# Attention scores by 64 keys and all eight heads at once, in place of 128 keys and four heads

## The chip, the cores and the metric

The kernel runs on one core of a Trainium2 chip. The metric is the device time of one execution in microseconds (us); of several runs the median is given. TensorE is PE in the profile (PEld are its weight loads), VectorE is DVE, ScalarE is ACT, GpSimd is POOL, SyncE is SP.

## The reference

Eight batches of 576 tokens and 8 heads of 64 columns. Attention looks back over a window of 128 tokens and subtracts a distance times a slope of its own for each head; its output goes through a layer that mixes all tokens of a batch.

```python
scores = scale * np.matmul(q, k.transpose(0, 1, 3, 2))
slopes = 2.0 ** (-8.0 * (np.arange(H, dtype=np.float32) + 1) / H)
bias = slopes[:, None, None] * (-np.abs(rel).astype(np.float32))[None, :, :]
mask = (rel >= 0) & (rel < window)
scores = np.where(mask, scores + bias[None], -1000000000.0)
attn = softmax(scores)
x = np.matmul(attn, v)                       # then (B, S, H * D)
wq, wk = x @ w_q, x @ w_k
W_tok = scale * np.einsum('bsd,btd->bst', wq, wk)
mixed = np.einsum('bst,btd->bsd', W_tok, x)
out = np.maximum(mixed, 0.0) @ w_out
```

All inputs and the output are float32 in DRAM. The kernel works in float16 on chip.

## The kernel before

**Steps of a batch.** Loads (Lq, Lk, Lv; Lt for the last 64 tokens of two batches) cast to float16 on the way and are issued by GpSimd (lines 504 to 523); four loads of the first batch come as float32 by SyncE and are cast on VectorE or ScalarE. TQ and TT transpose q and k on TensorE, two row halves at a time, with `flip` (lines 602 to 648), and ETQ and ETT copy them out of PSUM into `qkT`. `add_unit` (lines 654 to 690) makes a *unit*: QK, the scores of 128 keys against the 256 queries that can see them, for four heads (two pairs `a`, and in a pair the heads `e` on the two row halves of TensorE), laid out with keys on partitions; EXP, one exponential over 128x1024 on ScalarE from PSUM into a tile `pt`; MUL, one product on VectorE with a table `bias` that holds the exponential of the distance term, and zero outside the window. The last key block has 192 queries and takes the last 64 keys along in the other 64 columns (`segs`, table `biasl`). So a batch has four key blocks `g` of two units `u`, eight units in all.

`add_pv` (lines 694 to 739) makes PV for one tile of 128 queries: for each of eight heads two matmuls of 128 keys, `pt` as the stationary operand and 65 columns of `vt` (64 of v, and a column of ones that yields the sum of the softmax) as the moving one; X divides by that sum on VectorE (lines 729 and 730). There are five such tiles for a batch, the last with 64 queries. Then come XT (transposes of x, copied out by EXT), WQ, WK, G (the product of `wkn` and x), MX (mixing) with RM (the relu), and OUT with the copy EO and the store DO.

**Who orders the work.** `add` lists every step with its dependencies, its cost on the engines that may do it and a due time; `Order.solve` (line 234) plans them: of the steps that can start within 0.11 us of the earliest on an engine it takes the one with the smallest due time. The due times stand in the table `WANT`, one for each step, and the default for a step without entry follows `STRIDE` for the batch. `SWITCH` is the cost that the plan gives to a change of TensorE's array shape (`mode`). The engines then run their instructions in the planned order. Copies out of PSUM (ETQ, EXT, EWQ, EG, EO, RM and so on) go to ScalarE or VectorE as the plan finds best. While the planned start is below `WARM`, `keep_busy` fills gaps of TensorE with matmuls on a zero tile `fill`. Stores of batches 1 to 5 (`LATE`) wait until all loads are issued; their buffers are 23 (`HELD`).

**Buffers.** `nat` (q and k as loaded) and `vt` are four batches deep, `qkT`, `x` and what follows two, `pt` five key blocks of two tiles; PSUM has four pairs of banks, and QK, PV, TQ, XT and MX take a pair each. A v load of tile `t` waits only for the two PV that read that tile four batches before.

**The costs** that the plan uses for the steps at hand:

```python
s = add("QK", b, f"{g}.{u}", w, pe(0.225), need, em, banks=2, mode=1)
x = add("EXP", b, f"{g}.{u}", w + 0.6, {"ACT": (0.92, 1.02)}, [s, *oldp], ex, frees=[s])
mul[b, g, u] = add("MUL", b, f"{g}.{u}", w + 1.6, DVE(0.68), [x, (mkb if g < 3 else mkbl)[u]], ml)
p = add("PV", b, qt, want, pe(0.48 if qt else 0.25), need + [sets[b % NV], zerop], em, banks=2)
```

**The mask.** GpSimd makes an identity matrix, a table of distances (iota) and, after VectorE has cast it, sets everything outside the window to a large number in two selects; ScalarE makes `bias` from it with eight exponentials.

Of the kernel before, what the change touches and what calls it, by code (L numbers as in the profile page):

```python
# [14 lines left out]
P = 128  # L15
# [12 lines left out]
NPT = 5  # L28
PTW = 1088

# [3 lines left out]
STRIDE = 15.2  # L34
# [10 lines left out]
    "ident": -41.18, "idh": 86.52, "iota": -19.88, "dist": -5.89, "zeros": 80.97, "zerop":  # L45
# [237 lines left out]
def kernel(  # L283
# [137 lines left out]
    def mk_ident(o):  # L421
        make_identity(nc, ident32)
# [588 lines left out]
```

## Time and profile before

| What | Value |
|---|---|
| Median of 3 runs | 141.11 us (140.55 to 141.18) |
| Profiled execution | 141.34 us, of which its span in the profile 139.5 us |
| TensorE's granted clock | 0.997 |
| Busy in the span: PE, PEld, DVE, ACT, POOL | 129.3, 81.2, 112.6, 115.2, 110.0 us |
| EXP: 64 on ACT | 62.2 us busy, 1034 ns each |
| MUL: 48 and 16 on DVE | 32.0 and 10.8 us busy, 684 and 683 ns each |
| QK: 320 matmuls, 64\*128 pieces | 22.1 us booked |
| PV: 512 and 64 matmuls, 128\*128 | 22.9 and 4.9 us booked |
| Loads of v: 32 and 4 on POOL | 30.1 and 3.8 us busy |

The profile is one execution of the program. Times are from the start of the span. A group's row gives line, engine, operation, output and inputs, shapes and count, then busy time, the mean of one in ns, and the idle time of the engine ahead of it with what ended it. For matmuls the shape begins with the piece of the array that is used (rows\*columns). Matmuls are pipelined: their booked durations overlap, so that how fast they pass is read from their starts. A row of the timeline merges instructions of one group that follow each other: start, time from the first start to the last end, and the count.

### The profile page before, as it was taken

The numbers are of one execution on the slowest core, as the hardware profiler recorded it, in microseconds if no ns is written. First come the engines' busy times: TensorE is split into PE (matmuls) and PEld (weight loads), VectorE is DVE, ScalarE is ACT, GpSimd is POOL, SyncE is SP. The second block draws the span as 40 slices with busy tenths as digits, with TensorE's granted clock in tenths as the row PEclk, the third lists the DMA queues.
The fourth block names the chain that finished last, engine by engine and source line by source line (L and its number), as shares of the span: only waits on it lengthen the run. The fifth ranks groups of instructions, "written<-read, shape, count | busy, mean of one in ns | idle before, by whom it ended". The sixth has DMA issues, their size and how long they took to land.

```text
span 139.5 us, 5462 instructions
## 1 busy us (share of the span) xinstructions
PE 129.3 (93%) x2344; PEld 81.2 (58%) x2344; DVE 112.6 (81%) x250; ACT 115.2 (83%) x175; POOL 110.0 (79%) x145
## 2 busy tenths in 40 slices
PE   6999859998999999988999999999999999999980
PEld 2345447554676367766757567765666666865530
DVE  6648997659987899989999998899999989984400
ACT  6176988399669999999999989999999999676660
POOL 7899988899995899999999999999977745600000
PEclk9999999999999999999999999999999999999998
DMA  4999999999999999999999999999999993730494
GB/s 98 184 180 154 158 153 168 152 146 154 188 215 206 158 159 153 156 155 155 154 156 153 157 156 155 159 153 156 156 215 413 358 327 144 260 153 5 167 320 189
DMA packets 117127, 25.12 MB, mean 180 GB/s; under 512 B 113072, under 2 KB 114096, under 8 KB 117104
## 3 DMA queue, kind: packets, MB, share of 16 engines
q0 software_dynamic: 110912, 20.32, 169.0%
q1 hardware_dynamic: 6192, 4.46, 10.8%
q8 instruction: 18, 0.29, 0.8%
q14 instruction: 5, 0.04, 0.1%
HBM read 29.62 MB, written 9.44 MB: 280 GB/s over the span
## 4 chain that ended last, share of the span: by engine, by line
PE 60%; DVE 16%; POOL 8%; ACT 6%; DMA 5%; issue 2%; ACTq 0%; POOLq 0%; DVEq 0%
PE pair L344 52%; PE pair L347 8%; DVE pt L687 6%; DMA nat<-in_q_dram 5%; POOL nat L506 4%; ACT pt L680 4%; DVE x L730 3%; POOL vt L521 1%; POOL natt L513 1%; DVE inv L729 1%; DVE xtl L730 1%; DVE wqT L353 1%; DVE qkT L359 1%; DVE rm L843 1%; ACT xT L357 1%
## 5 line engine op out<-in xcount | busy, mean ns | idle before, releaser
L680 ACT ACTIVATE pt<-pair 128x1024 f16<-128x1024 f32 x64 | 62.2, 1034 | 2.3 <-PE pair L344 1.7
L687 DVE TENSOR_TENSOR pt<-pt,bias 128x1024 f16<-128x1024 f16 x48 | 32.0, 684 | 2.5 <-ACT pt L680 2.3
L344 PE MATMUL pair<-wout_sb,rm 128*128 128x512 f16 (+1 forms) x132 | 31.7, 373 | 0.2
L521 POOL DMA_DIRECT2D vt<-in_v_dram x32 | 30.1, 995 | 1.6 <-DMA natt<-in_q_dram 0.8
L506 POOL DMA_DIRECT2D nat<-in_k_dram x30 | 29.1, 997 | 0.5 <-DMA nat<-in_k_dram 0.3
L506 POOL DMA_DIRECT2D nat<-in_q_dram x30 | 29.0, 987 | 0.4 <-DMA natt<-in_k_dram 0.4
L344 PEld LDWEIGHTS <-pt 128*128 128x128 f16 x576 | 20.5, 97 | 6.2 <-issue 2.6
L344 PE MATMUL pair<-vt,pt 128*128 128x65 f16 x512 | 22.9, 193 | 0.4 <-ACT pt L680 0.4
L730 DVE TENSOR_TENSOR x<-pair,inv 128x512 f16<-128x512 f32 x32 | 22.1, 692 | 1.1
L344 PE MATMUL pair<-qkT 64*128 64x256 f16 (+2 forms) x320 | 22.1, 250 | 0.6 <-ACT pt L680 0.3
L351 ACT COPY osb<-pair 128x512 f32<-128x512 f32 x29 | 17.0, 596 | 5.7 <-PE pair L344 5.5
L344 PEld LDWEIGHTS <-rm 128*128 128x128 f16 x132 | 11.3, 97 | 11.8 <-issue 1.7
L357 ACT COPY qkT<-pair 128x1024 f32<-128x1024 f32 (+1 forms) x12 | 11.4, 949 | 7.7 <-PE pair L347 7.7
L344 PE MATMUL pair<-fill 128*128 128x512 f16 x52 | 15.4, 430 | 1.8 <-DVE fill L487 1.2
L918 POOL DMA_DIRECT2D out_dram<-osb x20 | 11.2, 574 | 6.6 <-ACT osb L351 3.6
L344 PEld LDWEIGHTS <-qkT 64*128 64x128 f16 x320 | 11.1, 94 | 8.0 <-issue 5.2
L347 PE MATMUL pair<-identh,nat 64*128 64x64 f16 x512 | 10.7, 190 | 1.3 <-DMA nat<-in_q_dram 0.9
L347 PEld LDWEIGHTS <-nat 64*128 64x128 f16 x512 | 9.2, 95 | 4.0 <-DMA nat<-in_q_dram 1.3
L687 DVE TENSOR_TENSOR pt<-pt,biasl 128x1024 f16<-128x1024 f16 x16 | 10.8, 683 | 0.0
L344 PE MATMUL pair<-xT,wqq_sb 128*128 128x320 f16 (+1 forms) x64 | 10.5, 286 | 0.3 <-DVE xT L359 0.3
L357 ACT COPY xT<-pair 128x512 f32<-128x512 f32 (+1 forms) x14 | 7.4, 527 | 3.6 <-PE pair L347 2.9
L359 DVE COPY qkT<-pair 128x512 f16<-128x512 f16 (+2 forms) x14 | 9.3, 686 | 1.3 <-PE pair L347 1.1
(63 smaller groups left out, 165.5 us busy)
## 6 DMA issues: line engine op xcount, KB each, us to landing
out_dram<-osb POOLq DMA_DIRECT2D x20, 256.0 KB, 4.6
vt<-in_v_dram POOLq DMA_DIRECT2D x32, 128.0 KB, 5.9
nat<-in_k_dram POOLq DMA_DIRECT2D x30, 128.0 KB, 6.0
nat<-in_q_dram POOLq DMA_DIRECT2D x30, 128.0 KB, 6.1
out_dram<-osb SPq DMA_DIRECT2D x11, 256.0 KB, 2.3
out_dram<-osb POOLq DMA_DIRECT2D x6, 128.0 KB, 4.2
natf<-in_q_dram SPq DMA_DIRECT2D x2, 256.0 KB, 4.7
natf<-in_k_dram SPq DMA_DIRECT2D x2, 256.0 KB, 5.4
```

What stands on the lines that cost most here:

```text
L344: hold(nc.tensor.matmul(*a, **k))
L347: hold(nc.tensor.transpose(*a))
L351: hold(nc.scalar.copy(out_ap, in_ap))
L353: hold(nc.vector.tensor_copy(out=out_ap, in_=in_ap))
L357: hold(nc.scalar.copy(out_ap.bitcast(FP32), in_ap.bitcast(FP32)))
L359: hold(nc.vector.tensor_copy(out=out_ap, in_=in_ap))
L506: return lambda: nc.gpsimd.dma_start(out=nat_s[b % NNAT][j][n], in_=src[b, :, P * n:P * n + P, :].transpose([1, 0, 2]))
L521: return lambda: nc.gpsimd.dma_start(out=vt_s[b % NV][t][:, :, 0:D], in_=v[b, :, P * t:P * t + P, :].transpose([1, 0, 2]))
L680: nc.scalar.activation(out=pt[:, 0:1024], in_=two(s.bank).rearrange("p e c -> p (e c)"), func=AF.Exp, scale=SCALE)
L687: ENG2[o.eng].tensor_tensor(out=pt[:, 0:1024], in0=pt[:, 0:1024], in1=bt, op=ALU.mult)
L730: nc.vector.tensor_tensor(out=x[r].rearrange("p (g h d) -> p g h d", g=2, h=4), in0=pxv[r, :, :, 0:64], in1=inv[r].unsqueeze(3).broadcast_ ...
L918: q.dma_start(out=out[b, P * st:P * st + P, c], in_=osb)
```

## The change

A unit now holds 64 keys against the 192 queries that can see them, for all eight heads: heads 0 to 3 on partitions 0 to 63, heads 4 to 7 on partitions 64 to 127, so 768 columns where there were 1024. QK uses 64x64 pieces of TensorE, four to a set (`x` the column half, `e` the row half). There are still eight units for a batch; the last takes key blocks 7 and 8 (128 and 64 queries). PV works by row halves: for each pair of head `h` and head `4 + h` two matmuls of 64 keys, four key blocks to a query tile. The tile `pt` is laid out with 64 zero columns ahead of each head's 192. v is loaded by head pairs with all tokens of the batch: four loads for a batch, each 64 partitions by 18 rows of 64, in place of four tiles of 128 tokens and a tail for two batches; every load of v waits for all PV of four batches before, and every PV waits for all four. The mask is made on VectorE by arithmetic in place of the selects on GpSimd, and the identity by a comparison of the iota with zero. All due times in `WANT` are new, `STRIDE` is 13.2 where it was 15.2. The rest of the batch (TQ, XT, WQ, WK, G, MX, OUT) stays.

```diff
-NPT = 5
+NPT = 10
+W = 192
-STRIDE = 15.2
+STRIDE = 13.2
...
+    def mk_idh(o):
+        nc.vector.tensor_scalar(out=identh, in0=wint[:, 0:P], scalar1=0.0, scalar2=1.0,
+                                op0=ALU.is_equal, op1=ALU.mult)
     def mk_dist(o):
-        nc.vector.tensor_copy(out=wm, in_=wint)
+        for x in range(2):
+            r = slice(64 * x, 64 * x + 64)
+            nc.vector.tensor_copy(out=wm[r], in_=wint[r, 64 * x:64 * x + W])
+        nc.vector.tensor_scalar(out=wlo, in0=wm, scalar1=-1.0e9, scalar2=0.0, op0=ALU.mult, op1=ALU.add)
+        nc.vector.tensor_scalar(out=whi, in0=wm, scalar1=-127.5, scalar2=1.0e9, op0=ALU.add, op1=ALU.mult)
+        nc.vector.tensor_tensor(out=wm, in0=wm, in1=wlo, op=ALU.max)
+        nc.vector.tensor_tensor(out=wm, in0=wm, in1=whi, op=ALU.max)
+        nc.vector.tensor_scalar(out=wm[64:128], in0=wm[64:128], scalar1=1.0 / 16.0, scalar2=0.0,
+                                op0=ALU.mult, op1=ALU.add)
...
+    def dma_v(b, t, x):
         return lambda: nc.gpsimd.dma_start(
-            out=vt_s[b % NV][t][:, :, 0:D],
-            in_=v[b, :, P * t:P * t + P, :].transpose([1, 0, 2]))
+            out=vt_s[b % NV][t][64 * x:64 * x + 64, :, :, 0:D],
+            in_=v[b, NHP * x + 2 * t:NHP * x + 2 * t + 2, :, :].rearrange("h (n t) d -> t (h n) d", t=64))
...
         def lv(t):
-            loads[b, "v", t] = load(("Lv", b, t), next(i), dma_v(b, t), 0.92, 0.87,
-                                    [oldv[t], oldv[t + 1], sets[b % NV]])
+            for x in range(2):
+                loads[b, "v", t, x] = load(("Lv", b, 2 * t + x), next(i), dma_v(b, t, x), 0.98, 0.98,
+                                           [*oldv, sets[b % NV]])
...
     def add_unit(b, g, u):
+        s = 2 * g + u
+        pt = pt_s[(8 * b + s) % NPT]
+        ptd = pt[:, 64:PTW].rearrange("p (e a c) -> p e a c", e=2, a=2)[:, :, :, 0:W]
         def em(o):
             for a in range(2):
-                hp = 2 * u + a
-                for kb, q0, wd, c0 in segs(g):
-                    for e in range(2):
-                        r = slice(64 * e, 64 * e + 64)
-                        mm(ps[:, e, 256 * a + c0:256 * a + c0 + wd],
-                                         t[r, 1, hp, P * kb:P * kb + P],
-                                         t[r, 0, hp, q0:q0 + wd], start=True, stop=True)
+                for sk, c0, n in ((s, 0, W),) if s < 7 else ((7, 0, P), (8, P, 64)):
+                    for x in range(2):
+                        for e in range(2):
+                            r = slice(64 * e, 64 * e + 64)
+                            mm(ps[64 * x:64 * x + 64, e, W * a + c0:W * a + c0 + n],
+                               t[r, 1, 2 * x + a, 64 * sk:64 * sk + 64],
+                               t[r, 0, 2 * x + a, 64 * sk:64 * sk + n], start=True, stop=True)
-        s = add("QK", b, f"{g}.{u}", w, pe(0.225), need, em, banks=2, mode=1)
+        q = add("QK", b, f"{g}.{u}", w, pe(0.175), [*need, *oldp], em, banks=2, mode=3)
         def ex(o):
-            nc.scalar.activation(out=pt[:, 0:1024], in_=two(s.bank).rearrange("p e c -> p (e c)"),
+            nc.scalar.activation(out=ptd, in_=two(q.bank)[:, :, 0:2 * W].rearrange("p e (a c) -> p e a c", a=2),
                                  func=AF.Exp, scale=SCALE)
         def ml(o):
-            ENG2[o.eng].tensor_tensor(out=pt[:, 0:1024], in0=pt[:, 0:1024], in1=bt, op=ALU.mult)
+            ENG2[o.eng].tensor_tensor(out=ptm, in0=ptm, in1=bt, op=ALU.mult)
...
     def add_pv(b, qt, want):
+        sv = [sk for sk in range(2 * qt - 2, 2 * qt + 2) if 0 <= sk < 9]
         def em(o):
-            for h in range(H):
-                kbs = [(qt - 1, False), (qt, True)] if qt else [(0, True)]
-                for i, (kb, cur) in enumerate(kbs):
-                    mm(px[:, h // 4, 65 * (h % 4):65 * (h % 4) + 65], ptc(kb, h, cur),
-                                     (vt_s[b % NV][kb] if kb < 4 else vtl_s[b // 2 % 2][:, b % 2])[:, h, 0:65],
-                                     start=(i == 0), stop=(i == len(kbs) - 1))
+            for a in range(2):
+                for e in range(2):
+                    for i, sk in enumerate(sv):
+                        ...
+                        for x in range(2):
+                            r = slice(64 * x, 64 * x + 64)
+                            h = 2 * a + e
+                            mm(px[:, x, 65 * h:65 * h + 65], pt_s[(8 * b + min(sk, 7)) % NPT][r, c:c + P],
+                               vt_s[b % NV][a][r, e, sk, 0:65],
+                               start=(i == 0), stop=(i == len(sv) - 1))
+        need += [loads[b, "v", t, x] for t in range(2) for x in range(2)]
+        p = add("PV", b, qt, want, pe(0.12 * len(sv)), list(dict.fromkeys(need)) + [sets[b % NV], *zerop], em, banks=2, mode=1)
```

More of the change, by code (lines that the diff above doesn't have):

```diff
@@ L44 @@
 WANT = {
-    "ident": -41.18, "idh": 86.52, "iota": -19.88, "dist": -5.89, "zeros": 80.97, "zerop":
[139 rows of a table removed]
+    "iota": -129.95, "idh": 70.52, "dist": 75.83, "zerop0": -109.3, "zerop1": 152.18, "bias":
[137 rows of a table added]
 }
@@ L301 @@
     fill = cpool.tile([P, 512], F16, name="fill")
-    ident32 = cpool.tile([P, P], FP32, name="ident32")
     identh = cpool.tile([P, P], F16, name="identh")
     wint = cpool.tile([P, 256], I32, name="wint")
-    wm = cpool.tile([P, 256], FP32, name="wm")
-    bias = [cpool.tile([P, 2, 2, 256], F16, name=f"bias{u}") for u in range(2)]
-    biasl = [cpool.tile([P, 2, 2, 256], F16, name=f"biasl{u}") for u in range(2)]
+    wm, wlo, whi = (cpool.tile([P, W], FP32, name=n) for n in ("wm", "wlo", "whi"))
+    bias = cpool.tile([P, 2, 2, W], F16, name="bias")
+    biasl = cpool.tile([P, 2, 2, W], F16, name="biasl")
     wqq_sb = cpool.tile([P, 4, P], F16, name="wqq_sb")
@@ L311 @@
     wout_sb = cpool.tile([P, 4, DM], F16, name="wout_sb")
-    qkT_s = [cpool.tile([P, 2, NHP, 640], F16, name=f"qkT{i}") for i in range(2)]
+    qkT_s = [cpool.tile([P, 2, NHP, S], F16, name=f"qkT{i}") for i in range(2)]
     nat_s = [[[cpool.tile([P, H, D], F16, name=f"nat{i}{j}{n}") for n in range(4)]
@@ L315 @@
     natt_s = [cpool.tile([P, 2, H, D], F16, name=f"natt{i}") for i in range(2)]
-    vt_s = [[cpool.tile([P, H, VW], F16, name=f"vt{i}{t}") for t in range(4)] for i in range(NV)]
-    vtl_s = [cpool.tile([P, 2, H, VW], F16, name=f"vtl{i}") for i in range(2)]
-    pt_s = [[cpool.tile([P, PTW], F16, name=f"pt{i}{u}") for u in range(2)] for i in range(NPT)]
+    vt_s = [[cpool.tile([P, 2, 9, VW], F16, name=f"vt{i}{j}") for j in range(2)] for i in range(NV)]
+    pt_s = [cpool.tile([P, PTW], F16, name=f"pt{i}") for i in range(NPT)]
     x_s = [[cpool.tile([P, DM], F16, name=f"x{i}{t}") for t in range(4)] for i in range(2)]
@@ L441, in em, with mk_zerop @@
             for t in vt_s[i]:
-                nc.vector.memset(t[:, :, D:D + 1], 1.0)
-            if i % 2 == 0:
-                nc.vector.memset(vtl_s[i // 2][64:128], 0.0)
-                nc.vector.memset(vtl_s[i // 2][:, :, :, D:D + 1], 1.0)
-        return em
-    def mk_zeros(o):
-        for t in qkT_s:
-            nc.vector.memset(t[:, :, :, S:640], 0.0)
-    def mk_zerop(o):
-        for i in range(NPT):
-            for u in range(2):
-                nc.vector.memset(pt_s[i][u][:, 1024:PTW], 0.0)
+                nc.vector.memset(t[:, :, :, D:D + 1], 1.0)
+        return em
+    def mk_zerop(i):
+        def em(o):
+            for t in pt_s[i::2]:
+                nc.vector.memset(t[:, 0:1024].rearrange("p (n c) -> p n c", c=256)[:, :, 0:64], 0.0)
+                nc.vector.memset(t[:, 1024:PTW], 0.0)
+        return em
     def mk_pads(o):
@@ L467, in mk_wqq, with mk_bias @@
             nc.vector.tensor_copy(out=wqq_sb[:, :, 64 * e:64 * e + 64], in_=wq_sb)
-    def mk_bias(u):
-        def em(o):
-            for h in range(4 * u, 4 * u + 4):
-                hp, e = divmod(h, 2)
-                nc.scalar.activation(out=bias[u][:, e, hp % 2, :], in_=wm, func=AF.Exp,
-                                     scale=-(2.0 ** (-(h + 1))))
-        return em
-    def mk_biasl(u):
-        def em(o):
-            src = bias[u].rearrange("p e a c -> p (e a) c")
-            dst = biasl[u].rearrange("p e a c -> p (e a) c")
-            for c, n in ((0, 192), (192, 64)):
-                nc.vector.tensor_copy(out=dst[:, :, c:c + n].bitcast(FP32), in_=src[:, :, 0:n].bitcast(FP32))
-        return em
+    def mk_bias(o):
+        for e in range(2):
+            for a in range(2):
+                nc.scalar.activation(out=bias[:, e, a, :], in_=wm, func=AF.Exp, scale=-(2.0 ** (-(2 * a + e + 1))))
@@ L487, with mk_biasl @@
+    def mk_biasl(o):
+        src = bias.rearrange("p e a c -> p (e a) c")
+        dst = biasl.rearrange("p e a c -> p (e a) c")
+        for c, n in ((0, P), (P, 64)):
+            nc.vector.tensor_copy(out=dst[:, :, c:c + n].bitcast(FP32), in_=src[:, :, 0:n].bitcast(FP32))
     nc.vector.memset(fill, 0.0)
-    ident = add("ident", "", "", -299, {"POOL": (0.58, 0.6)}, [], mk_ident)
-    idh = add("idh", "", "", -290, DVE(0.27), [ident], mk_dve)
     iota = add("iota", "", "", -300, {"POOL": (0.34, 0.34)}, [], mk_iota)
-    dist = add("dist", "", "", -300, DVE(0.4), [iota], mk_dist)
@@ L492 @@
-    zeros = add("zeros", "", "", 0, DVE(0.55), [], mk_zeros)
-    zerop = add("zerop", "", "", -59, DVE(0.45), [], mk_zerop)
-    mask = add("mask", "", "", -298, {"POOL": (0.86, 0.86)}, [dist], mk_mask)
-    mkb = [add("bias", u, "", -240 + 10 * u, ACT(1.35), [mask], mk_bias(u)) for u in range(2)]
-    sets = [add("ones", i, "", -200 + 20 * i, DVE(0.5), [], mk_ones(i)) for i in range(NV)]
+    idh = add("idh", "", "", -290, DVE(0.29), [iota], mk_idh)
+    dist = add("dist", "", "", -300, DVE(1.6), [iota], mk_dist)
@@ L497 @@
+    zerop = [add("zerop", i, "", -59, DVE(0.55), [], mk_zerop(i)) for i in range(2)]
+    mkb = add("bias", "", "", -240, ACT(1.14), [dist], mk_bias)
+    sets = [add("ones", i, "", -200 + 20 * i, DVE(0.25), [], mk_ones(i)) for i in range(NV)]
     pads = add("pads", "", "", -297, ACT(1.3), [], mk_pads)
-    mkbl = [add("biasl", u, "", 6, DVE(0.55), [mkb[u]], mk_biasl(u)) for u in range(2)]
+    mkbl = add("biasl", "", "", 6, DVE(0.4), [mkb], mk_biasl)
     nat, natt, vt = {}, {}, {}
@@ L571, in lt @@
                                        [tt.get(pr - 2)]) for j in range(2)]
-        def lvt():
-            pr = b // 2
-            if b % 2 == 0:
-                loads[b, "v", 4] = loads[b + 1, "v", 4] = load(
-                    ("Lv", b, 4), next(i), dma_vtail(pr), 0.92, 0.87,
-                    [pvd.get((b - 4, 4)), pvd.get((b - 3, 4)), sets[b % NV]])
         if b == 0:
@@ L583, in add_loads @@
             lq(0, 2), lq(1, 2), lq(0, 3), lq(1, 3)
-            lv(0), lv(1), lt(), lv(2), lv(3), lvt()
+            lv(0), lv(1), lt()
         else:
@@ L670, in add_unit @@
         need = [evt[b, g], evt[b, g + 1]] if g < 3 else [evt[b, 3], ett[b]]
[L671 to L673 removed]
+        prev = 8 * b + s - NPT
         oldp = []
         if prev >= 0:
[L676 to L677 removed]
+            pb, ps = divmod(prev, 8)
+            oldp = [pvd[pb, ps // 2], pvd[pb, ps // 2 + 1]]
+        q = add("QK", b, f"{g}.{u}", w, pe(0.175), [*need, *oldp], em, banks=2, mode=3)
@@ L679, in ex @@
+        qkd[b, g, u] = q
         def ex(o):
-            nc.scalar.activation(out=pt[:, 0:1024], in_=two(s.bank).rearrange("p e c -> p (e c)"),
+            nc.scalar.activation(out=ptd, in_=two(q.bank)[:, :, 0:2 * W].rearrange("p e (a c) -> p e a c", a=2),
                                  func=AF.Exp, scale=SCALE)
-        x = add("EXP", b, f"{g}.{u}", w + 0.6, {"ACT": (0.92, 1.02)}, [s, *oldp], ex, frees=[s])
-        bt = (bias if g < 3 else biasl)[u].rearrange("p e a c -> p (e a c)")
+        x = add("EXP", b, f"{g}.{u}", w + 0.6, {"ACT": (0.71, 0.81)}, [q, *oldp], ex, frees=[q])
@@ L686, in ml @@
+        bt = (bias if s < 7 else biasl).rearrange("p e a c -> p (e a) c")
+        ptm = ptd.rearrange("p e a c -> p (e a) c")
         def ml(o):
-            ENG2[o.eng].tensor_tensor(out=pt[:, 0:1024], in0=pt[:, 0:1024], in1=bt, op=ALU.mult)
-        mul[b, g, u] = add("MUL", b, f"{g}.{u}", w + 1.6, DVE(0.68),
-                           [x, (mkb if g < 3 else mkbl)[u]], ml)
+            ENG2[o.eng].tensor_tensor(out=ptm, in0=ptm, in1=bt, op=ALU.mult)
+        mul[b, g, u] = add("MUL", b, f"{g}.{u}", w + 1.6, DVE(0.55), [x, mkb if s < 7 else mkbl], ml)
@@ L692 @@
     ENG2 = {"DVE": nc.vector, "POOL": nc.gpsimd}
     def add_pv(b, qt, want):
-        def ptc(kb, h, cur):
-            hp, e = divmod(h, 2)
-            u, a = divmod(hp, 2)
-            g = min(kb, 3)
-            o = 512 * e + 256 * a + (192 if kb == 4 else 0)
-            if not cur:
-                o += 128
-            if qt == 4 and b % 2:
-                o -= 64
-            return pt_s[(4 * b + g) % NPT][u][:, o:o + P]
+        sv = [sk for sk in range(2 * qt - 2, 2 * qt + 2) if 0 <= sk < 9]
@@ L716, in add_pv @@
-        need = [mul[b, g, u] for g in gs for u in range(2)]
-        need += [loads[b, "v", t] for t in ({max(qt - 1, 0), qt})]
-        p = add("PV", b, qt, want, pe(0.48 if qt else 0.25), need + [sets[b % NV], zerop], em, banks=2)
+            for a in range(2):
+                for e in range(2):
+                    for i, sk in enumerate(sv):
+                        c = 64 + 256 * (2 * e + a) + 64 * (2 * qt - sk)
+                        if sk == 8:
+                            c += P
+                        if qt == 4 and b % 2:
+                            c -= 64
+                        for x in range(2):
[4 more added lines that the diff above has]
+                               start=(i == 0), stop=(i == len(sv) - 1))
@@ L719, in add_pv @@
+        need = [mul[b, min(sk, 7) // 2, sk % 2 if sk < 8 else 1] for sk in sv]
+        need += [loads[b, "v", t, x] for t in range(2) for x in range(2)]
+        p = add("PV", b, qt, want, pe(0.12 * len(sv)), list(dict.fromkeys(need)) + [sets[b % NV], *zerop], em, banks=2, mode=1)
         pvd[b, qt] = p
```

25 lines of the change are left out of this document (2 added, 23 removed), and 276 rows, old and new, of the table WANT.

## The prediction

> **What bounds the kernel now.** I read the page first, then busy time by stretches, then the groups with shapes kept apart, then the timelines of TensorE and ScalarE, and last the issue order of the loads.
>
> ```profile
> span 139.5 us, 5462 instructions
> PE 129.3 (93%) x2344; PEld 81.2 (58%) x2344; DVE 112.6 (81%) x250; ACT 115.2 (83%) x175; POOL 110.0 (79%) x145
> PE 60%; DVE 16%; POOL 8%; ACT 6%; DMA 5%; issue 2%; ACTq 0%; POOLq 0%; DVEq 0%
> ```
>
> The chain that ended last lies to 60% on PE, but not on PE alone. The stretches (us, then busy PE, PEld, DVE, ACT, POOL, clock, DMA) say why:
>
> ```profile
> 55.00:70.00 15.00, 13.97 (x316) 10.26 (x313) 13.88 (x28) 14.43 (x21) 15.00 (x18) 1.00 2.42 155
> 70.00:85.00 15.00, 14.81 (x315) 9.50 (x314) 13.81 (x27) 14.19 (x23) 15.00 (x19) 1.00 2.42 156
> 85.00:100.00 15.00, 14.56 (x296) 9.80 (x295) 13.94 (x29) 14.20 (x20) 15.00 (x19) 1.00 2.43 157
> 115.00:136.00 21.00, 20.50 (x297) 12.60 (x293) 13.12 (x27) 14.97 (x30) 4.33 (x8) 1.00 0.49 174
> ```
>
> In the middle four engines are within 7% of full at once: ACT 95%, DVE 92%, POOL 100% (it issues loads), PE 97%. Busy PE isn't streaming PE: a 65-column matmul is booked with 193 ns, while sixteen of them pass in 0.64 us, one per 30 ns. The timeline shows the difference:
>
> ```profile
> 60.88 0.42 PE L344 MATMUL pair<-vt,pt 128*128 128x65 f16 x8
> 61.23 0.39 PE L344 MATMUL pair<-qkT 64*128 64x256 f16 x4
> 61.83 0.64 PE L344 MATMUL pair<-vt,pt 128*128 128x65 f16 x16 [0.20 <-ACT pt L680]
> 62.68 0.45 PE L344 MATMUL pair<-wqT,gs 64*128 64x512 f16 x6 [0.20 <-DVE x L730]
> 63.57 0.39 PE L344 MATMUL pair<-wqT,gs 64*128 64x512 f16 x2 [0.44 <-DVE x L730]
> ```
>
> Eight PV matmuls stream for 0.25 us, yet the QK unit behind them starts 0.35 us after the first: 0.10 us goes when the shape of the array changes (128\*128 to 64\*128). That QK unit streams two steps of 0.11 us, as its matmuls run in pairs on the two row halves; the next PV starts 0.60 us after it, so 0.28 us beyond stream and switch is waiting for the exponentials (ACT). So PE is the chain, with ACT and DVE pulling at it. Counting starts in the trace from 30 to 130 us: 77 us of columns at 0.417 ns, some 102 changes of shape at 0.12 us (12), 3 us of small losses, and about 6 us of waits in 26 places over 160 ns. A batch takes 14.9 us: 11.5 of columns, 1.8 of switches, 0.6 lost, 0.9 waited.
>
> Ahead of this lies a start that the loads set (TQ, the transposes of q and k, of batch 1 come at 26.64, behind seven fill matmuls); behind it, from 108 us, an end where the last load landed at 105.8 and PE still has 28 us of work, about two batches.
>
> ```profile
> 25.02 1.68 PE L344 MATMUL pair<-fill 128*128 128x512 f16 x7
> 26.64 0.64 PE L347 MATMUL pair<-identh,nat 64*128 64x64 f16 x32
> ```
>
> **The change, part by part.** The rows that price it:
>
> ```profile
> L680 ACT ACTIVATE pt<-pair 128x1024 f16<-128x1024 f32 x64 | 62.2, 1034 | 2.3 <-PE pair L344 1.7 <-DVE pt L687 0.3
> L687 DVE TENSOR_TENSOR pt<-pt,bias 128x1024 f16<-128x1024 f16 x48 | 32.0, 684 | 2.5 <-ACT pt L680 2.3
> L359 DVE COPY xT<-pair 128x1024 f16<-128x1024 f16 x5 | 3.4, 680 | 0.0
> L359 DVE COPY xT<-pair 128x256 f16<-128x256 f16 x5 | 1.4, 284 | 0.5 <-PE pair L347 0.5
> L473 ACT ACTIVATE bias<-wm 128x256 f16<-128x256 f32 x8 | 2.6, 402 | 0.1
> L344 PEld LDWEIGHTS <-wkn 128*64 128x64 f16 x80 | 3.7, 109 | 1.4 <-ACT wkn L351 0.6 <-issue 0.5 <-DVE inv L729 0.2
> L344 PEld LDWEIGHTS <-qkT 64*128 64x128 f16 x320 | 11.1, 94 | 8.0 <-issue 5.2 <-ACT qkT L357 1.3 <-ACT rm L841 0.4
> ```
>
> *EXP and MUL.* Still 64 of each, 768 columns for 1024. ACT from 256 to 1024 columns: (1034 - 402) / 768 = 0.82 ns a column, so 0.21 us less for each, 13.5 us in all. DVE by its f16 copies: (680 - 284) / 768 = 0.52 ns, 0.13 us less, 8.5 us in all. From 26.6 to 136 us, 56 of each: ACT 97.5 busy to 85.7, DVE 92.2 to 84.8. Neither is the chain alone, so this pays only through PE's waits.
>
> *QK.* A unit becomes eight 64x64 matmuls of 192 columns in two sets of four: 2 x 80 = 160 ns if all four pieces run at once, for 218 now. Seven batches of eight units after 26.6 us: 56 x 0.055 = -3.1 us. That rows pair is in the QK rows, that column halves pair is in G (x,wkn, eight 256-column matmuls of 128\*64 within 0.63 us); both at once no row shows, so the bounds are -3.1 and, with only two pieces at once (320 ns a unit), 56 x 0.102 = +5.7; I take -3.1, as each kind of pair has a row.
>
> *PV.* 16 matmuls per query tile become 32 on row halves, in pairs. Pairs on row halves at this width are in the trace: 32 TQ transposes of 64 columns start within 0.64 - 0.19 = 0.45 us, 29 ns a pair. Per batch 72 steps of 31 ns become 68 pairs of 30 (the last tile needs three key blocks): -0.19, over seven batches -1.3 us.
>
> *Changes of shape.* QK gets a shape of its own, PV joins the transposes' and MX's. QK next to TQ, XT or MX now switches, PV next to them no longer does: I take 0, with two a batch either way as bounds, 14 x 0.12 = 1.7 us.
>
> *Loads.* The 32 v loads of 1024 pieces (a piece is 64 elements) and four v tails become 32 of 1152: the same 36,864 pieces. POOL starts one load per 0.87 us, a tail shape of 1024 pieces per 0.81; for 1152 I take 0.91, bounds 0.86 and 0.98. Sum: 36 issues took 31.0 us, 32 take 29.1 (27.5 to 31.4). POOL also loses ident and both masks with the wait before them, 2.1 us.
>
> *Start.* Behind the last q/k load of batch 1 (issued 18.1 to 19.9, landed 25.2) POOL saves 2.1 and one tail (0.8), pays 4 x 0.1 for v and about 0.6 as a weight load moves ahead of it: -1.9; batch 0's own chain ends near 25.0 and caps it: -1.5 (0 to -1.9). PV0.0 now waits for all four v loads instead of one. By the new due times they are among the first ten issued, so they land near 16.5, and PV0.0 ran at 16.4: nothing, or 1 us off the start if late, with PE's queue behind it (QK of the next units, then EXP). The mask moves to seven DVE operations of 0.2 to 0.3 us between the casts of q and k; bias on ACT shrinks from eight to four; the first MUL came at 13.5, and all this was done by 9.5: nothing, covered.
>
> *Waits.* With ACT and DVE an eighth and a twelfth lighter, PE's 6 us of waits shrink. If all stayed: 0; if all went: -6.0. I take two thirds, -4.0, as PE stays the chain but ACT falls from 95 to about 90% of the shorter stage.
>
> *The rest:* nothing. The waits of QK for freed pt tiles lie behind a PV that precedes them on PE anyway; pt is as deep (640 keys); memsets swap one for another.
>
> **Sum** against the profiled execution's 141.34 us (span 139.5 and 1.84 around it): -1.5 - 3.1 - 1.3 - 4.0 = -9.9, 131.4. The median of the runs is 0.2 lower, so 131.2. Bounds without a rival: all favourable -1.9 - 3.1 - 1.3 - 1.7 - 6.0 = 127.1; no gain in waits or start and more switches: 138.4.
>
> **The rivals.**
>
> *A: weight loads pace the QK pieces.* A set of four needs four 64-column loads in 80 ns. The 128\*64 load stands with 109 ns where others take 94 to 97, some 12 to 15 ns more. The pipelined loads of TQ (64 rows, 128 columns) pass one per 15 ns, so one of these could cost 15 + 12 = 27 ns; four in a row make a set 107. A batch has 18 sets (seven units of two, one of four): 18 x 107 = 1.93 us for 1.28, over seven batches +4.5: 135.7. For: the row. Against: G hides two such loads in a 109 ns step.
>
> *B, the slower side: the pieces take turns.* If loads and matmuls of the four quadrants follow one another, a set costs 4 x 37 ns or more. It decides from there: break-even is 9.9 / 7 = 1.4 us more a batch, 2.7 us for 18 sets, 149 ns a set. G allows up to 54 ns a load (two in a 109 ns step); at 54, 18 x 216 = 3.9 us a batch, +18.2: 149. With two pieces at a time, +8.8 against the sum, it is 140.0, still hardly faster. Against it: matmuls on either kind of halves start 4 to 7 ns apart.
> The Trainium skill ("TensorEngine Tiling (Array Packing)", Restrictions) says that column tiling disables Fast Weight Load; with the load formula of "TensorE: Matmul & The Clock Gate" (LDWEIGHTS), columns over 1.2, a piece's load is an estimated 53 ns, and the time about B's 149 if the loads follow one another. The trace agrees with the first half only as far as the wkn row stands higher; none of its rows shows loads of several pieces in a row.
>
> *C: the loads pace the front.* POOL is 100% busy from 47.7 to 100.7 us and the last q/k landed 3 us ahead of its TQ. If v loads go at 18/16 of their full 0.995, 1.12 us, they cost +4.8, less 2.1 on POOL: the last load lands at 108.5 and TQ7 starts near 110 instead of 108. Batch 7's own 13.5 us, 3 of latencies that nothing fills any more and the 5.3 behind PE's last matmul give 132, or 135 if some OUT work is still left then. Against: 28 us of backlog hid this before, and some 18 are left.
>
> **How the numbers follow.** The forecast 0.62, A 0.13, C 0.09, B 0.13, and 0.03 for two pieces at a time. Less than 0.5% (0.7 us) is what a measurement here can't tell from no change. The forecast, A and C are faster, two pieces at a time, near that bound, is put down as the same, B is slower: 0.84, 0.03, 0.13. The range 127.0 to 138.5 takes in the forecast's bounds, A and C, and leaves out the other two.
>
> **What would show it.** EXP rows of 768 columns near 0.82 us (768 x 0.82 ns below 1.03 to 0.82), MUL near 0.55; eight QK matmuls with the next block 160 to 180 ns after the first plus a switch; 32 PV matmuls in 0.48 us; TQ of batch 1 near 25; waits of PE for ACT and DVE down; last load near 103. QK sets of over 100 ns mean A, over 149 B; PE idle before TQ for a DMA late in the run means C. PE's waits unchanged with lighter ACT would make the largest term wrong.

## The result and the profile after

The kernel after takes 156.87 us (median of 4 runs, 155.66 to 158.27), the kernel before 140.97 beside it: ratio 1.110, interval 1.102 to 1.119. It is slower by 15.9 us, where 131.2 was forecast and 138.5 was the upper end. The profiled execution took 156.27 us. Here and below medians take in every run, while ratios and their intervals take only the runs in the chip's faster state.

The page of the kernel after, its busy times, the granted clock by slices and the chain that ended last:

```profile
span 154.5 us, 6981 instructions
...
PE 132.8 (86%) x3112; PEld 82.7 (54%) x3112; DVE 104.6 (68%) x252; ACT 103.9 (67%) x169; POOL 105.2 (68%) x137
...
PEclk9999999999998799699999789999999999999999
...
PE 68%; DVE 11%; issue 8%; ACT 6%; DMA 3%; SPq 0%; ACTq 0%; DVEq 0%
```

ACT and DVE are lighter, as planned, and POOL too. The two new things are the PE count, 3112 matmuls for 2344 (and as many weight loads), and "issue", 8% of the chain for 2%: time in which an engine waits for nothing that the profile shows. The same stretches as before:

```profile
55.00:70.00 15.00, 10.63 (x325) 8.06 (x325) 9.82 (x22) 7.57 (x11) 14.21 (x17) 0.89 2.69 151
70.00:85.00 15.00, 12.89 (x353) 8.07 (x350) 12.50 (x27) 12.67 (x21) 14.57 (x18) 1.00 2.55 153
85.00:100.00 15.00, 13.50 (x333) 9.08 (x333) 9.08 (x22) 9.79 (x17) 13.10 (x16) 0.89 2.41 150
115.00:136.00 21.00, 20.77 (x583) 13.84 (x578) 18.88 (x42) 17.41 (x28) 10.20 (x19) 1.00 0.64 222
```

From 55 to 70 us PE is busy for 10.63 of 15 us (13.97 before) and ACT for 7.57 (14.43): nobody is full except POOL, which still issues loads. From 115 us, with the loads over, PE is as full as before. The last TQ of batch 1 started at 27.86 us (26.64 before) and the last of batch 7 at 123.20 (108.09); from there to the end it is 31.3 us (31.4). So the loss is 1.2 us at the start, 13.9 in the stretch with loads, none behind it. The timeline of PE in that stretch, kernel after:

```profile
59.27 0.28 PE L341 MATMUL pair<-vt,pt 64*128 64x65 f16 x7 [0.20 <-DVE x L699]
62.82 0.65 PE L341 MATMUL pair<-vt,pt 64*128 64x65 f16 x17 [3.27 <-issue]
...
67.49 0.27 PE L341 MATMUL pair<-qkT 64*64 64x192 f16 x3
68.47 0.65 PE L341 MATMUL pair<-qkT 64*64 64x192 f16 x21 [0.70 <-issue]
```

PE stops in the middle of a PV, whose operands were all there, for 3.27 us, and in the middle of a QK unit for 0.70. Counted in the trace, PE's instructions (matmuls and weight loads together) break off at the 193rd and then only at every 256th behind it: 11 stops of 0.3 to 3.5 us, 12.5 us in all. The kernel before has the same places and loses nothing there. The DMA queue of the instructions, before and then after (packets, MB, share):

```profile
q8 instruction: 18, 0.29, 0.8%
```

```profile
q8 instruction: 24, 0.39, 1.0%
```

Six packets more of 16 KB, 64 bytes for each of 256 instructions: PE's own stream, 6226 instructions (weight loads included) for 4690. Where PE stops, it goes on 1.3 to 1.7 us behind the end of the packet that brings its next block. The Trainium skill ("Runtime: NRT & Kernel Launch", Instruction fetch mechanics) says that an engine fetches its instructions in 16 KiB blocks of 256 while it executes, and that crossing a block is mostly hidden. The trace agrees with the block, and not with "hidden": up to 3.5 us for one crossing here.

The granted clock falls as well; the digits 6 to 8 of PEclk show it. It is 0.50 in three stretches of 3.4 us, which begin at 49.1, 62.8 and 86.7 us, that is from 0.1 us ahead of the end of the three longest stops (48.06, 62.82, 86.49) to 1.0 behind it. In the second, the 32 transposes of a TQ take 1.04 us where they took 0.64 before the stop:

```profile
58.43 0.64 PE L344 MATMUL pair<-identh,nat 64*128 64x64 f16 x32
64.72 1.04 PE L344 MATMUL pair<-identh,nat 64*128 64x64 f16 x32
```

The three stretches cost 5.1 us at the most (an estimate: half of 3 x 3.4). The kernel before has none until 138.6 us. That the stops bring them about is not shown: among the runs below, split16 has a stop of 1.1 us and pv_merge one of 1.6 with none behind them, and pad_tiny has a stretch from 19.7 us with no such stop ahead of it.

In the waits (us in all, times, longest) the same shows as "issue", first before and then after; the long one is new:

```profile
PEld L344 <- issue: 18.0, 65, 0.6
```

```profile
PEld L341 <- issue: 25.0, 58, 3.4
...
PE pair L341 <- issue: 7.7, 7, 3.3
```

The pieces of the change themselves, in the groups (busy, mean ns) and in the timeline of the kernel after:

```profile
L651 ACT ACTIVATE pt<-pair 128x768 f16<-128x768 f32 x64 | 48.9, 821 | 4.6 <-PE pair L341 4.2
...
L659 DVE TENSOR_TENSOR pt<-pt,bias 128x768 f16<-128x768 f16 x56 | 29.9, 551 | 5.7 <-ACT pt L651 5.3
```

```profile
114.53 0.54 PE L341 MATMUL pair<-vt,pt 64*128 64x65 f16 x24
114.99 0.36 PE L341 MATMUL pair<-qkT 64*64 64x192 f16 x8
115.28 1.04 PE L341 MATMUL pair<-wout_sb,rm 128*128 128x512 f16 x4
```

EXP 821 ns and MUL 551 are what the prediction had (0.82, 0.55). Twelve PV pairs and a switch take 0.46 us (0.36 + 0.10); a QK unit and a switch 0.29 (0.33 in the kernel before). The four pieces of a set start 3 to 4 ns apart. A set inside a run of QK passes in 82 ns (median), but the first set of a run in 107; before, a step of two matmuls took 109 ns and the first of a run 120.

### The profile page after: what moved, and what is told of

It is laid out like the page before. It is cut to its first block, busy times and chain, and to the rows that moved or that the text cites. A ratio compares the mean times of both kernels' runs of the same rounds, so it can differ in the third digit from the quotient of the medians.

```text
span 154.5 us, 6981 instructions
## 1 busy us (share of the span) xinstructions
PE 132.8 (86%) x3112; PEld 82.7 (54%) x3112; DVE 104.6 (68%) x252; ACT 103.9 (67%) x169; POOL 105.2 (68%) x137
## 4 chain that ended last, share of the span: by engine, by line
PE 68%; DVE 11%; issue 8%; ACT 6%; DMA 3%; SPq 0%; ACTq 0%; DVEq 0%
PE pair L341 59%; PE pair L344 9%; ACT pt L651 3%; DVE x L699 3%; DMA natf<-in_k_dram 3%; DVE pt L659 3%; ACT qkT L354 1%; DVE rm L812 1%; DVE qkT L356 1%; DVE inv L698 1%; ACT xT L354 1%; ACT osb L348 1%; DVE osb L350 1%; DVE xT L356 1%; DVE xtl L699 0%
## 5 line engine op out<-in xcount | busy, mean ns | idle before, releaser
L651 ACT ACTIVATE pt<-pair 128x768 f16<-128x768 f32 x64 | 48.9, 821 | 4.6 <-PE pair L341 4.2
L659 DVE TENSOR_TENSOR pt<-pt,bias 128x768 f16<-128x768 f16 x56 | 29.9, 551 | 5.7 <-ACT pt L651 5.3
L341 PE MATMUL pair<-vt,pt 64*128 64x65 f16 x1088 | 23.6, 193 | 6.6 <-issue 6.0
L341 PEld LDWEIGHTS <-pt 64*128 64x128 f16 x1088 | 20.3, 95 | 11.7 <-issue 9.1
L341 PE MATMUL pair<-qkT 64*64 64x192 f16 (+2 forms) x576 | 19.7, 247 | 2.5 <-issue 1.3
L354 ACT COPY qkT<-pair 128x1024 f32<-128x1024 f32 (+1 forms) x17 | 16.0, 941 | 7.8 <-PE pair L344 6.4
L341 PEld LDWEIGHTS <-qkT 64*64 64x64 f16 x576 | 11.3, 109 | 12.2 <-issue 6.9
L698 DVE RECIPROCAL inv<-pair 128x8 f32<-128x8 f32 (+1 forms) x40 | 8.1, 203 | 10.5 <-PE pair L341 10.2
L812 DVE TENSOR_SCALAR rm<-pair 128x512 f16<-128x512 f32 x16 | 10.6, 685 | 0.8 <-PE pair L341 0.6
L341 PE MATMUL pair<-xT,wqq_sb 128*128 128x256 f16 (+1 forms) x64 | 11.0, 293 | 0.1
```

The lines of the kernel that those rows point to most:

```text
L341: hold(nc.tensor.matmul(*a, **k))
L354: hold(nc.scalar.copy(out_ap.bitcast(FP32), in_ap.bitcast(FP32)))
L651: nc.scalar.activation(out=ptd, in_=two(q.bank)[:, :, 0:2 * W].rearrange("p e (a c) -> p e a c", a=2), func=AF.Exp, scale=SCALE)
L659: ENG2[o.eng].tensor_tensor(out=ptm, in0=ptm, in1=bt, op=ALU.mult)
L698: nc.vector.reciprocal(out=inv[r], in_=pxv[r, :, :, 64])
L812: hold(nc.vector.tensor_scalar(out=out_ap, in0=in_ap, scalar1=0.0, scalar2=WSCALE, op0=ALU.max, op1=ALU.mult))
```

## The experiments

Three theories at the outset. F: PE runs dry because its instructions arrive in blocks and it uses them up faster. L: PE waits for v, since every PV now waits for four loads. O: the new order or the 64x64 pieces are slow in themselves. "Idle at block ends" below is counted in each trace as above.

| Run | PE instructions | idle at block ends, us | median, us | ratio to before (interval) |
|---|---|---|---|---|
| before | 4690 | 0 | 140.97 | |
| after | 6226 | 12.5 | 156.87 | 1.110 (1.102 to 1.119) |
| pv_merge | 5138 | 6.8 | 148.94 | 1.054 (1.043 to 1.064) |
| both_merge | 4562 | 2.2 | 143.50 | 1.014 (1.003 to 1.024) |
| v_once | 6226 | 6.8 | 148.20 | 1.051 (1.041 to 1.061) |
| pad_tiny | 6210 | 3.6 | 161.59 | 1.145 (1.136 to 1.155) |
| split16 | 5330 | 2.5 | 144.56 | 1.024 (1.020 to 1.029) |
| split32 | 6610 | 8.2 | 152.43 | 1.083 (1.080 to 1.086) |
| exp768 | 4690 | 0 | 139.16 | 0.989 (0.983 to 0.995) |
| both_light | 4562 | 1.2 | 139.07 | 0.987 (0.985 to 0.990) |
| both_v | 4562 | 1.0 | 141.42 | 1.005 (1.001 to 1.008) |
| before_v | 4690 | 0 | 140.96 | 1.001 (0.997 to 1.005) |
| before_cheap | 4690 | 0 | 138.85 | 0.985 (0.983 to 0.988) |

**Fewer instructions in the new kernel.** pv_merge makes one PV matmul of 130 columns for two heads, both_merge also one QK matmul of 384 columns for two; the columns that PE streams are the same, and so is the order.

```diff
-                            mm(px[:, x, 65 * h:65 * h + 65], pt_s[...][r, c:c + P], vt_s[b % NV][a][r, e, sk, 0:65],
+                            mm(px[:, x, 130 * a:130 * a + 130], pt_s[...][r, c:c + P], vt_s[b % NV][a][r, :, sk, 0:65],
```

```diff
-                               t[r, 0, 2 * x + a, 64 * sk:64 * sk + n], start=True, stop=True)
+                               t[r, 0, 2 * x:2 * x + 2, 64 * sk:64 * sk + n], start=True, stop=True)
```

pv_merge: 

> The changed kernel, but PV takes one matmul of 130 columns for the two heads of a pair where it takes two of 65, with the first head's probabilities for both (this part of the computation is changed). Columns streamed, pairing, waits, loads and order stay; TensorE's instructions fall from 6226 to 5138, 642 a batch. Theory F (TensorE runs out of instructions: they come in blocks of 256, the next block is usable about 5.8 us after the one before was begun while loads run): 2.5 blocks x 5.8 = 14.5 us a batch in the load phase, for 17.6; about 140 us (136 to 144), and the idle spells at block ends shrink. Theory L (PV waits for the late v loads, which it now needs all four) and theory O (the new order or the pieces of the array are slow themselves): nothing they name is changed, 155 to 158 us.

both_merge: 

> As pv_merge, and QK also takes one matmul of 384 columns where it takes two of 192, with one head's keys for two heads (this part is changed too). Columns, waits, loads and order stay; TensorE's instructions are 4562, fewer than the 4690 of the kernel before: 570 a batch, 12.9 us in blocks of 5.8. F: the blocks no longer set the pace, the spells at block ends are gone, the clock stays near 1.0, and the sum of the prediction holds: 131 to 134 us. L and O: 155 to 158 us, with PV waiting on v landings as before.

Measured: 156.9, 148.9 and 143.5 us, falling with the count, and the idle time at block ends with it (12.5, 6.8, 2.2). Neither v nor the steps' order changed, and the pieces take nearly the same time: two sets of 192 columns 107 + 82 ns, one of 384 columns 191; the PV of a tile with the switch behind it 503 ns as 32 matmuls, 463 as 16. So L and O don't explain 13.4 of the 15.9 us. But both runs miss F's ranges, by 4.9 and 9.5 us: the time stays 12 us above the forecast even with the stalls nearly gone. The last big stop in both_merge, in a TQ that had begun:

```profile
56.78 0.21 PE L344 MATMUL pair<-identh,nat 64*128 64x64 f16 x3
58.05 0.78 PE L344 MATMUL pair<-identh,nat 64*128 64x64 f16 x29 [1.06 <-issue]
```

It has fewer instructions than the kernel before and still stalls here: what counts is how fast PE gets through a single block, not the total.

**Fewer loads.** v_once takes out the v loads of batches 1 to 7.

```diff
-                loads[b, "v", t, x] = load(("Lv", b, 2 * t + x), next(i), dma_v(b, t, x), 0.98, 0.98,
+                loads[b, "v", t, x] = load(("Lv", b, 2 * t + x), next(i), dma_v(b, t, x) if b == 0 else (lambda: None), 0.98, 0.98,
-                               vt_s[b % NV][a][r, e, sk, 0:65],
+                               vt_s[0][a][r, e, sk, 0:65],
```

> The changed kernel, but v is loaded for the first batch alone and used for all (this part is changed): 28 of the 106 loads are left out, and no PV after the first batch waits for one. Instructions of TensorE stay at 6226. F: the q and k loads still stand in the queues until about 78 us and blocks come late until then; after it the blocks come in time: 145 to 152 us. L: the waits for v are gone, 131 to 135 us. O: 155 to 158 us.

148.2 us: in F's range, and not in L's or O's. L falls by the trace of the kernel after, too: there PE's matmuls wait for a load of v once, for 0.2 us. With the same instructions half of the idle time at block ends goes; the rest lies before 76 us, where loads still run, but for 0.7 us. In the kernel after a fetch starts 2 to 4.5 us behind the crossing of the block before while loads run, and 0 to 1.5 us without them, but once 3.4 (in the kernel before 1.3 to 4.7 while loads run). So the loads take part as what holds up the fetch, and not as v that comes late. The waits of v_once:

```profile
PE pair L341 <- issue: 4.0, 3, 2.0
```

**More instructions in the old kernel.** pad_tiny puts 19 one-column matmuls behind each PV of the kernel before.

```diff
+            for i in range(19):
+                mm(px[:, i % 2, 300 + i:301 + i], fill[:, 0:P], fill[:, 0:1], start=True, stop=True)
```

> The kernel before, with 19 matmuls of a single column behind each PV into unused PSUM columns: TensorE's instructions rise from 4690 to 6210, as many as in the changed kernel; loads, order and waits stay. Their own time is 760 x 12 to 25 ns, 9 to 19 us. F: idle spells of 0.5 to 3 us appear at every 256th instruction while loads run, and 17.6 us a batch there as in the changed kernel: 160 to 175 us. L and O: their own time alone, 150 to 160 us, and no idle spells at fixed instruction numbers.

161.6 us lies in F's range, but proves little: the tiny matmuls pass one per 25 ns, so they are some 19 us of work themselves (40 PV x 19 x 25 ns) and stretch the blocks. Idle at block ends 3.6 us. A cleaner version cuts the old QK matmuls into pieces that run at the same time: split16 into 64x64 pieces, split32 these once more by columns.

```diff
-                        mm(ps[:, e, 256 * a + c0:256 * a + c0 + wd], t[r, 1, hp, P * kb:P * kb + P],
-                                         t[r, 0, hp, q0:q0 + wd], start=True, stop=True)
+                    for y in range(2):    # split16: 1
+                        n = wd // 2       # split16: wd
+                        ...
+                                mm(ps[64 * x:64 * x + 64, e, c:c + n], t[r, 1, hp, k:k + 64],
+                                   t[r, 0, hp, q0 + n * y:q0 + n * y + n], start=True, stop=True)
```

split16: 

> The kernel before, in its own order, with one change: each QK matmul of 64*128 and 256 columns is split into two 64*64 pieces on the column halves, so that a unit is 16 matmuls for 8, four running at once. 5330 instructions of PE for 4690; the columns that PE streams stay. A batch holds 666 for 586, 2.6 blocks of 256. Theory F (PE runs dry where its instructions have not arrived): at 5.8 us a block that is 15.1 us a batch, over the 13.6 us that batches 1 to 7 take before, so stalls at every 256th instruction, 3 to 8 us in all, 144 to 149. Theory O (the new order or the 64*64 pieces cost the time) : order unchanged, and if the pieces are at fault each unit grows by tens of ns: 141 to 143 with the idle time inside QK units and none at the 256th instructions. Theory L (late v loads): 141.

split32: 

> As the run before, and each piece is cut again into two halves of its columns (128 each), so 32 matmuls a unit for 8 and 6610 instructions of PE, 826 a batch or 3.2 blocks of 256. Theory F: 18.7 us a batch while loads run, stalls of 12 to 18 us in all at the 256th instructions, 154 to 162. Theory O: stalls only within QK units, below 0.1 us each, so at most 147. Theory L: 141 to 143.

144.6 and 152.4 us: F's first range is hit, partly by luck, and its second missed by 1.6: there is less idle time at block ends than the 3 to 8 and 12 to 18 expected; O and L are out of both. Old order, old loads, old columns, and the stops appear at the 193rd and every 256th instruction behind it, where the kernel before has none. split32 in the middle of a QK unit, split16 in the middle of a TQ, which the edit does not touch:

```profile
52.99 0.44 PE L344 MATMUL pair<-qkT 64*64 64x96 f16 x27
55.76 0.23 PE L344 MATMUL pair<-qkT 64*64 64x32 f16 x5 [2.33 <-issue]
```

```profile
43.20 0.40 PE L347 MATMUL pair<-identh,nat 64*128 64x64 f16 x15
44.66 0.43 PE L347 MATMUL pair<-identh,nat 64*128 64x64 f16 x17 [1.06 <-issue]
```

Not all of it is idle time at block ends: 8.2 of 11.6 us for split32, 2.5 of 3.7 for split16. The pieces themselves are not slower in split32: inside a run a set of 128 columns takes 56 ns, one of 256 in split16 109. Behind the longest stop split32 also has a stretch at half the clock (from 56.6 us, 1.7 us at the most).

**What lighter EXP, MUL and QK are worth.** exp768 narrows EXP and MUL in the old kernel, both_light in both_merge, before_cheap QK as well in the old kernel (the first turn of the buffers is full in each).

```diff
+            n = 1024 if prev < 0 else 768
-            nc.scalar.activation(out=pt[:, 0:1024], in_=two(s.bank).rearrange("p e c -> p (e c)"),
+            nc.scalar.activation(out=pt[:, 0:n], in_=two(s.bank).rearrange("p e c -> p (e c)")[:, 0:n],
-            ENG2[o.eng].tensor_tensor(out=pt[:, 0:1024], in0=pt[:, 0:1024], in1=bt, op=ALU.mult)
+            ENG2[o.eng].tensor_tensor(out=pt[:, 0:n], in0=pt[:, 0:n], in1=bt[:, 0:n], op=ALU.mult)
```

exp768: 

> The kernel before, in its own order, with EXP and MUL over 768 of the 1024 columns from the sixth key block on (the last 256 columns keep older values, so two of the eight heads are not computed): ACT 0.21 us and DVE 0.13 us less for each of 54 units, as in the kernel after. It measures the term of -4.0 us for the waits of PE by itself. If lighter ACT and DVE shrink PE's waits as the prediction took it: 137 to 138, bound 135. If PE's waits come from the fixed order (an operand of one step made just ahead of it on a short path) and not from the load on ACT and DVE: 140 to 141.5.

both_light, with `ptd[:, :, 0]` and every second head of `ptm` in place of all: 

> The kernel after with PV and QK merged as in both_merge (143.5 us), and EXP and MUL over 384 of the 768 columns from the eleventh unit on (four of the eight heads keep older values): ACT 0.31 us and DVE 0.20 us less for each of 54 units. If the some 10 us of waits of PE that are left in both_merge come from the load on ACT and DVE: most of them go, 135 to 138. If they come from the order in which the steps stand on PE: 141 to 143.5.

before_cheap:

```diff
+        cut = 4 * b + g >= NPT and g < 3
-                for kb, q0, wd, c0 in segs(g):
+                for kb, q0, wd, c0 in [(g, P * g, 192, 0)] if cut else segs(g):
```

> The kernel before in its own order, with the change's lighter work but none of its instructions added: from batch 1's second key block on, QK, EXP and MUL of key blocks 0 to 2 take 192 of the 256 queries (the other 64 columns keep older values), 40 units of the 64. If the prediction's terms hold where the order stays: 40 x 0.055 = -2.2 for QK and 40 of 54 units' share of the -1.7 that lighter EXP and MUL brought in exp768, -1.2, so 137.5 (136.5 to 138.5). If lighter QK only turns into longer waits at fixed places: 139 to 140.5.

exp768: 139.2, between the two expectations. The change's own relief of ACT and DVE is worth 1.5 us (ratio 0.989), not 4. The waits of PE in the kernel before and in exp768 show why: those for `pt`, which EXP writes, shrink, and those for `x` (behind PV) are 0.6 and 0.9.

```profile
PE pair L344 <- ACT pt L680: 1.2, 4, 0.5
...
PE pair L344 <- DVE x L730: 0.6, 2, 0.4
PE pair L344 <- ACT qkT L357: 0.4, 2, 0.2
PE pair L344 <- ACT xT L357: 0.3, 2, 0.2
```

```profile
PE pair L344 <- DVE x L732: 0.9, 2, 0.5
PE pair L344 <- ACT pt L681: 0.8, 2, 0.5
PE pair L344 <- ACT qkT L357: 0.4, 2, 0.2
PE pair L344 <- ACT xT L357: 0.4, 2, 0.2
```

before_cheap adds the lighter QK and comes to 138.9, ratio 0.985: 2.1 us, between its two expectations again (3.4, or 0.4 to 1.9), though close to the second. QK's 2.2 us and EXP's 1.2 do not add up: part of the room is waited away. both_light: 139.1, between its two expectations (135 to 138, 141 to 143.5) and 4.4 us below both_merge, of which 1.0 is idle time at block ends and up to 1.7 a stretch at half the clock (from 58.3 us) that only both_merge has. The waits counted in its trace are 7.3 us for 10: about a quarter went with a relief one and a half times the change's own (0.31 us a unit on ACT for 0.21), on top of it: the load on ACT and DVE has a share in them, and not the larger one.

**The loads in either order.**

both_v (both_merge with the edit of v_once): 

> The kernel after with PV and QK merged as in both_merge (143.5 us) and v loaded for batch 0 alone, so 28 of 106 loads are not made (all batches use the v of batch 0). In both_merge some 10 us of waits of PE are left after 24 us, and its last load lands near 101. If the pace of the loads sets these waits (rival C of the prediction): 136 to 139. If they come from the order of the steps and the short paths between PE, ACT and DVE in it: 141.5 to 143.5, with the waits near 9 to 10 us and only the rest of the block-end stalls (2.2 us) gone.

before_v (the same edit in the kernel before): 

> The kernel before with v loaded for batch 0 alone (28 of its loads of v and 3 of 4 v tails not made). It says what the loads are worth in the old order: if they pace it, 136 to 138.5; if the order and PE do, 140 to 141. It is the counterpart of both_v: the same edit on the other order.

141.4 and 141.0: about what the order of the steps was to give (141.5 to 143.5, 140 to 141), and not the pace of the loads. The old order gains nothing from 28 v loads less (ratio 1.001, 0.997 to 1.005), the new one 2.1 us, of which 1.2 are idle time at block ends; both_merge's stretch at half the clock is gone too. Waits of over 250 ns after 24 us (a start of PE later than what streams before it explains), outside block ends, are 10.4 us in both_v and 10 in both_merge (6.4 in the kernel before). So the loads don't make them. In both_merge they are these:

```profile
PE pair L344 <- ACT pt L651: 1.4, 4, 0.4
PE pair L344 <- DVE x L697: 1.3, 4, 0.4
...
PE pair L341 <- ACT pt L651: 0.9, 2, 0.6
PE pair L341 <- DVE rm L810: 0.8, 2, 0.4
PE pair L341 <- ACT qkT L354: 0.5, 1, 0.5
```

They are the old kind of wait, for `pt`, `x`, `qkT` and `rm`, and there are more of them: 23 for 17.

## Why the prediction was wrong

*The step that failed* is "The rest: nothing". The change adds 768 matmuls and as many weight loads, and these were counted only as columns and switches. PE has a second pace, that of its instructions. In the kernel after, while loads run, one block takes 2 to 4.5 us until its fetch starts, about 0.9 for the packet and 1.3 to 1.7 until PE goes on, some 5.8 us. What decides is how long PE takes for each single block. In the kernel before this was 5.0 us or more for every block while loads ran, and none ended in a stop. In the kernel after eight blocks of that stretch went by in 2.5 to 4.7 us, and seven of them ended in a stop; of the seven that took 5.4 us or more two did. By batch: the kernel before has 586 instructions, 2.3 blocks, in the 13.6 us that a batch took there (81.5 / 6, from TQ of batch 1 to TQ of batch 7), 5.9 us a block. The kernel after has 778, 3.04 blocks, and was to pass them in 12.4 us (13.6 less 8.4 / 7), 4.1 us a block. It took 15.9 us a batch (95.3 / 6), 5.2 us a block; the 17.6 us of 3.04 x 5.8 are too much, as not every block ends in a stop. The counts stood in the page of before, in the instructions of PE and the 18 packets of the instruction queue.

*The sum, term by term.* PV (-1.3) was priced right as work, pairs in 30 ns, and EXP and MUL came as forecast. QK (-3.1) was nearly right: sets of four take 82 ns, but the first of a run takes some 25 more, where the first step of a run took some 10 more before; over 34 runs behind TQ of batch 1 (39 before) that is about 0.5 us. A change of shape takes 95 to 98 ns in either kernel, but behind TQ of batch 1 there are 118 of them for 106: some 1.1 us more where the sum had 0, within its bounds. The other two terms failed:

- Start, -1.5: TQ of batch 1 came at 27.86, 1.2 us later than before, and in both_merge at 26.43. The last q/k load of batch 1 landed at 24.7, only 0.5 us earlier. It was issued at 19.46, 0.45 later than before, as POOL had waited 1.6 us for earlier loads to land (0.52, 0.23 and 0.83 before the issues at 11.55, 12.66 and 17.70). And TQ was released by EXP, not by a load:

```profile
27.86 0.64 PE L344 MATMUL pair<-identh,nat 64*128 64x64 f16 x32 [0.37 <-ACT pt L651]
```

- Waits, -4.0: in the old order the same relief is worth 1.5; in the new order the waits rose by 3.6 (10 us for 6.4, both_merge). The step "ACT falls from 95 to about 90%, so two thirds go" took the waits for a matter of load. They stand at fixed places of the order, where one step's operand is made just ahead of it.

The forecast was 131.2. Of the 25.7 us to 156.9, 13.4 are the instructions that both_merge takes out (10.3 of idle time at block ends, and two of the three stretches at half the clock, 3.4 at the most) and 2.1 what both_v takes out besides; the waits' 7.6 (3.6 instead of -4.0) and the start's 1.3 (both_merge) make 24.4, and the switches' 1.1 and QK's 0.5 make 26.0. All but the first two are read from the traces; no run set them apart from each other.

*The rivals.* The slower side came true by another mechanism than B's. B and A fall: pieces do not take turns, and a set inside a run takes 82 ns. Only the first of a run takes the 107 that A had for all of them, and B needed 149 for all. C falls as a pace: the last load landed at 106.2 (105.8 before, 103 forecast), but taking 28 loads away moves both orders by little. Two pieces at a time falls with the sets.

*What stays open.* Why the new order has 23 such waits where the old one had 17: no run exchanged the orders of the two kernels with the work kept. Nor do the runs show why a fetch starts later while loads run, or what sets the clock to half.

## What to carry to other kernels

Splitting matmuls into smaller pieces that run at the same time keeps PE's columns and doubles its instructions: count these in blocks of 256 with weight loads, and look at how long PE will take for each block. With loads in flight, as measured here, most blocks that PE passed in under 5 us ended in a stop; the kernel before had none so short. An idle PE with "issue" as the releaser in the middle of a step whose operands are there is the sign, and equal distances in instructions are the proof. And an engine that becomes lighter shortens only the waits for its own results: in a hand-ordered kernel, count those places before crediting the rest.

## What the runs showed of the hardware

- PE stopped for 0.3 to 3.5 us at ends of blocks of 256 instructions, in kernels of both layouts, mostly while loads ran.
- The kernel after lost more than the length of its stops: the granted clock was 0.50 for 3.4 us about the end of each of the three longest (0.89 over 55 to 70 us), where the kernel before had 1.00 until 138.6 us. That the stops cause this is not shown.
- Matmuls of one column on the whole array passed one per 25 ns (pad_tiny), pieces that run at the same time, on row halves or quarters, start 3 to 4 ns apart at the least.
- 64x64 pieces of 192 columns run four at a time with their weight loads mostly hidden: 82 ns a set inside a run (the columns alone 80), 107 for the first set. Sets of 128 columns inside a run take 56 ns (split32). QK took 27.95 us there, from each run's start to that of what follows, for 21.1 in split16 with the same columns; 5.8 of the 6.8 us between them are stops at block ends that fall into QK, the one shown above among them.
